# A planned kernel's order redone: q's sixteen transfers as single jobs, one conversion step as two jobs, the first pair's squares on ScalarE, twelve softmax products on GpSimd

## The chip, the cores and the metric

The kernel runs on one core of a Trainium2 chip. The metric is the device time of one execution in microseconds (us), lower is better. Engines are named as in the profile: PE is TensorE's matmul side, PEld its weight load, DVE is VectorE, ACT is ScalarE, POOL is GpSimd, SP is SyncE, which in this kernel computes nothing and issues every DMA in order.

## The reference, cut to what matters

Local attention over chunks of 64 tokens, then two MLPs, all on 4608 tokens (8 batches of 576) with 512 channels (8 heads of 64):

```
scores = scale * q_c @ k_c^T                  # within a chunk of 64 tokens
attn   = exp(scores - max)
attn   = attn / (attn.sum(-1) + 1e-9)
x = (attn @ v_c) -> [4608, 512]
h = relu(x @ w_in)                            # 512 -> 2048
x = (h * h) @ w_out                           # 2048 -> 512
gate = sigmoid(x @ w_gate); val = x @ w_val   # 512 -> 1536
out = (gate * val) @ w_out2                   # 1536 -> 512
```

Inputs arrive in 64-bit words; the weights are turned into float32 on the chip by several instructions of ACT, DVE and POOL.

## The kernel before, in words

The program is not written in the order in which it runs. Python code creates jobs (a job is one engine's work with its inputs and outputs), a planner gives each job a due time, counted back from the nominal times of the matmul jobs, and walks through time placing jobs on the engines and buffers in one large arena of SBUF. The chip then executes the order that came out, one fixed queue per engine, with semaphores for every dependence. What the chip sees of a change of the planner's inputs is thus an order and a choice of buffers.

The attention is done for 36 tiles of 128 tokens. For a tile, PE transposes k and q (line 816; from tile 12 on DVE turns q instead, out of a buffer `ql`), makes the scores S (L836), DVE takes the maximum and subtracts it (L862, L864), ACT takes the exponential (L867), DVE sums it (L868), adds the 1e-9 (L871), takes the reciprocal (L872) and multiplies the 128x512 tile by it (L873). PE transposes the result (T, L880), ACT copies it out of PSUM (`aT`, L427), PE multiplies by v (X, L896), and ACT writes the result into `raw` (L914). The table `TIMES` holds a nominal time for k, q, S, T and X of each tile.

Three tiles make a block of 384 tokens, two blocks make a pair; there are six pairs. The first product (512 -> 2048) runs pair by pair, in eight groups of weights. The first pair is done plainly, 32 output blocks; each is read out of PSUM by ACT with a relu into a buffer `e`, squared, and stored to DRAM (`gd`). The other pairs use seven products for eight, with sums and differences of inputs and outputs (`B..`, `T..` are token operands, `wia`, `wit`, `wis`, `wid` weight operands, `b`, `c`, `e`, `h` output buffers that are stored to `gd`). Every operand is kept as a high and a low part, the low part made by DVE (L447), and each product is three passes (L649, three matmuls of 128x384). Weights `w` are made from `wraw` by ACT (L489, L493), DVE (L496, L498, L505) and POOL (L512). While one pair's products run, the attention of the next pair is threaded between them, so PE alternates between L649 and the attention's lines. From about 360 us on there is no attention left. A later stage (L1031) then does the rest.

`ql` is filled by `load_turned`: sixteen small transfers, one for each head pair and quarter of the partitions, that were one job. There are eleven such fillings. `gd<-e` and the like are the stores of an output buffer, also issued by SP; a buffer is written again only after its store has landed. `ACTF.Square` is ACT's square, `binary("DVE", ..., ALU.mult, ...)` the same on DVE with one operand in PSUM (L456).

Of the kernel before, what the change touches and what calls it, by code (L numbers as in the profile page):

```python
# [39 lines left out]
class Buf:  # L40
    def __init__(self, size=0, top=False, name="", psum=False, op=False):
        self.size, self.top, self.name, self.psum, self.op = size, top, name, psum, op
        self.writers, self.readers, self.users = [], [], 0
        self.at = None


class Job:
    __slots__ = ("eng", "cost", "emit", "deps", "succ", "left", "bufs", "allocs", "lag",
                 "n", "due", "nominal", "start", "end", "stream", "bytes", "look", "started", "shared")


class Plan:
# [3 lines left out]
    def job(self, eng, cost, emit, reads=(), writes=(), stream=None, size=0, soon=None, look=None, at=None, shared=False):  # L56
        j = Job()
        j.shared = shared
# [9 lines left out]
        for b in writes:  # L68
            j.deps.update(b.writers)
            j.deps.update(b.readers)  # L70
# [11 lines left out]
        j.allocs = [b for b in writes if (b.size or b.psum) and b.users == 1]  # L82
# [6 lines left out]
    def due(self):  # L89
# [29 lines left out]
    def run(self):  # L119
# [105 lines left out]
        while done < len(jobs):  # L225
            moved = True
            while moved:
                moved = False
                for e in engines:
# [23 lines left out]
                    while ready[e] and tries < 600:  # L253
# [5 lines left out]
                        if need and ok:  # L259
                            if due - t + shift > (j.look or (self.LOOK if e == "SP" else self.NEAR)):  # L260
                                ok = False
                            else:
                                held = 0
                                for d, m in wants:
                                    if d >= due or d > t - shift + self.HOLD:
                                        break
                                    if not jobs[m].started:
                                        held += sum(b.size for b in jobs[m].allocs if b.at is None)
# [69 lines left out]
def tile_attention_relu2_glu(  # L338
# [77 lines left out]
    def dma(out_, in_, reads=(), writes=(), size=0, n=1, soon=None, look=None):  # L416
# [5 lines left out]
        return job("SP", 0.45 * n, go, reads, writes, size=size, soon=soon, look=look)  # L422
# [46 lines left out]
    def to_float32(src, name, look=None, raws=None):  # L469
# [24 lines left out]

        def three():
            nc.vector.tensor_scalar_max(at(w), at(w), TINY)  # L496
# [19 lines left out]
        job("DVE", 0.8, three, [w], [w], shared=True)  # L516
# [193 lines left out]
    LOOK_QK = 40.0  # L710
# [18 lines left out]
    def load_turned(nm, g):  # L729
# [4 lines left out]
        def both():  # L734
            x = at(r).rearrange("p (h i d) -> p h i d", h=HP, d=32)
            o, i = [], []
            for g4 in range(4):
                part = slice(32 * g4, 32 * g4 + 32)
                cols = slice(32 * (g4 % 2), 32 * (g4 % 2) + 32)
                for hp in range(HP):  # L740
                    o.append(x[part, hp])
                    i.append(src[b, 2 * hp + g4 // 2, s:s + GROUP * 32, cols].rearrange("(i t) d -> t i d", t=32))
            return o, i

        dma(lambda: both()[0], lambda: both()[1], writes=[r], size=P * HP * GROUP * 32 * 8, n=16, look=LOOK_QK)

    def turn_round(nm, t, o):
# [23 lines left out]
        (-2.5, -2.25, 3.5, 9.5, 12.5),  # L771
        (2.25, -4.75, 24.5, 15, 5.5),
        (5.75, 10.25, 5.75, 10.25, 19.75),
        (11.75, 7.5, 13, 28.5, 24.75),
        (22.25, 18.5, 20.5, 17, 37),
        (41.25, 44.75, 41.75, 42.5, 50.75),
        (64.25, None, 63, 73.5, 74.5),
        (78, None, 77.5, 81.5, 83.25),
        (84, None, 82, 89, 94.25),
        (101, None, 98, 106.75, 106),  # L780
        (84.75, None, 93.5, 122.25, 108.25),
        (105.25, None, 107.5, 105.75, 110.5),
        (125, None, 120, 125.75, 142),
        (113, None, 119.5, 124.5, 127.25),
        (125, None, 128, 150.75, 155.75),
        (146.781, None, 147.822, 153.027, 157.191),
        (152.75, None, 158.5, 160, 170),
        (158.5, None, 163.5, 167, 183.5),
        (182.75, None, 185.25, 192.5, 190.25),
        (192.25, None, 192.5, 200, 194.75),  # L790
        (197.25, None, 199.5, 203.25, 209),
        (194.75, None, 201.5, 203.25, 200),
        (205.25, None, 211.25, 219.75, 219.75),
        (216.5, None, 225.25, 234.75, 229),
        (247, None, 242.75, 254.5, 261.5),
        (259.5, None, 253.75, 269.25, 275.25),
# [594 lines left out]
```

## Time and profile before

| | |
|---|---|
| median of 3 runs | 1624.57 us (1623.97 to 1626.49) |
| the profiled execution's own time | 1623.55 us |
| its span | 1621.5 us (2.05 us lie outside the span) |
| mean granted clock of PE | 0.995 of full speed |
| PE busy | 1590.0 us, 98% of the span |
| DVE busy | 1325.2 us, 82% |
| ACT busy | 971.5 us, 60% |
| POOL busy | 524.8 us, 32% |

Busy is the time in which an engine executed an instruction, over one profiled execution. The span begins at the first and ends at the last instruction. In a row of a timeline, the bracket at the end holds the idle time of that engine just before the instruction and what ended it.

### The profile page before, as it was taken

The page shows a single profiled execution, that of the slowest core. Times are in us where ns is not written, and L with a number is a line of the kernel's source. Part 1 is how long each engine was busy: PE and PEld are TensorE (multiplying, and loading weights), DVE is VectorE, ACT ScalarE, POOL GpSimd, SP SyncE. Part 2 cuts the span into 40 slices and gives each one's busy share as a digit, 9 for nine tenths or more (in the row PEclk, how much of TensorE's full clock was granted, in tenths as well). Part 3 has the DMA queues.
Part 4 walks back from the last instruction along what each step waited for, and adds up shares of the span by engine and source line. Part 5 has one row for each costly group of instructions (what it writes and reads, how often), then busy time and mean ns, then how long its engine had stood idle before and what let it go on. Part 6 is the DMA issues. An engine that isn't in the chain of part 4 may idle for free.

```text
span 1621.5 us, 30663 instructions
## 1 busy us (share of the span) xinstructions
PE 1590.0 (98%) x10500; PEld 1442.0 (89%) x10500; DVE 1325.2 (82%) x2290; ACT 971.5 (60%) x1968; POOL 524.8 (32%) x420
## 2 busy tenths in 40 slices
PE   7999999999999999999999999999999999999998
PEld 5898998999999999999998898888888888888887
DVE  7997977878899999999998696835776748889886
ACT  7875756666776666566665555534564545555553
POOL 0253402030442114021157685624676531000000
PEclk9999999999999999999999999999999999999999
DMA  9874667676885676686787556486536577876562
GB/s 219 248 182 117 155 162 189 192 199 198 278 283 194 216 239 201 217 283 209 256 282 262 192 174 228 157 270 230 174 145 218 184 260 252 235 193 169 144 171 47
DMA packets 390796, 333.34 MB, mean 206 GB/s; under 512 B 234736, under 2 KB 325616, under 8 KB 390640
## 3 DMA queue, kind: packets, MB, share of 16 engines
q1 hardware_dynamic: 390640, 331.38, 67.0%
q8 instruction: 83, 1.36, 0.3%
q14 instruction: 73, 0.60, 0.1%
HBM read 209.13 MB, written 122.16 MB: 204 GB/s over the span
## 4 chain that ended last, share of the span: by engine, by line
PE 73%; DVE 2%; issue 1%; POOL 1%; ACT 0%; DMA 0%; SPq 0%; DVEq 0%; POOLq 0%; ACTq 0%
PE bank L1031 37%; PE bank L649 35%; PE bank L896 0%; PE bank L836 0%; DMA w__5725<-wf 0%; POOL ws__5872 L456 0%; POOL ws__5810 L456 0%; DVE T__1990 L447 0%; PE bank L880 0%; DMA g__6317<-gd 0%; POOL ws__7199 L456 0%; DVE T__1983 L447 0%; DVE b__4956 L456 0%; ACT c__3874 L427 0%; POOL wf__7139 L512 0%
## 5 line engine op out<-in xcount | busy, mean ns | idle before, releaser
L512 POOL TENSOR_TENSOR wf__6765<-wf__6765,wr__6689 128x512 int32<-128x512 int32 x18 | 36.4, 2023 | 170.0 <-DVE wf__6765 L505 52.7
L512 POOL TENSOR_TENSOR wf__3460<-wf__3460,wr__3365 128x512 int32<-128x512 int32 x16 | 21.5, 1341 | 172.5 <-DVE wf__3460 L505 65.9
L512 POOL TENSOR_TENSOR wf__7139<-wf__7139,wr__6689 128x512 int32<-128x512 int32 x18 | 28.0, 1558 | 115.4 <-DVE wf__7139 L505 73.6
L456 POOL TENSOR_TENSOR raw__501<-raw__677,raw__501 128x384 f32<-128x384 f32 x20 | 23.5, 1192 | 37.4 <-ACT raw__677 L914 14.2
L493 ACT ACTIVATE wr__6689<-wr__6689 128x512 int32<-128x512 uint32 x36 | 24.0, 667 | 0.0
L447 DVE TENSOR_TENSOR wx__7277<-ws__7199,wx__7277 128x512 fp32r<-128x512 f32 x18 | 19.0, 1054 | 3.9 <-ACT wx__7277 L442 3.9
L447 DVE TENSOR_TENSOR wx__7082<-ws__7199,wx__7082 128x512 fp32r<-128x512 f32 x18 | 18.0, 999 | 4.9 <-ACT wx__7082 L442 4.9
L496 DVE TENSOR_SCALAR wf__7139<-wf__7139 128x512 f32<-128x512 f32 x18 | 11.9, 659 | 7.0 <-ACT wf__7139 L489 7.0
L456 POOL TENSOR_TENSOR ws__7199<-ws__7199,wf__6765 128x256 f32<-128x256 f32 x18 | 16.2, 898 | 1.3
L496 DVE TENSOR_SCALAR wf__6765<-wf__6765 128x512 f32<-128x512 f32 x18 | 11.5, 641 | 6.1 <-ACT wf__6765 L489 6.0
L489 ACT ACTIVATE wf__3460<-wr__3365 128x512 f32<-128x512 f32 x16 | 10.7, 670 | 9.2 <-DMA wf<-wf__3460 6.3
L456 POOL TENSOR_TENSOR ws__7199<-wf__6765,wf__7139 128x256 f32<-128x256 f32 x18 | 15.5, 863 | 0.3
L505 DVE SCALAR_TENSOR_TENSOR wf__7139<-wr__6689,wf__7139 128x512 int32<-128x512 int32 x18 | 15.4, 856 | 0.2
L442 ACT ACTIVATE wx__7204<-wf__7139 128x256 fp32r<-128x256 f32 x18 | 7.4, 413 | 12.2 <-POOL wf__7139 L512 12.2
L447 DVE TENSOR_TENSOR wx__7204<-wf__7139,wx__7204 128x256 fp32r<-128x256 f32 x18 | 14.0, 778 | 0.6 <-ACT wx__7204 L442 0.5
L496 DVE TENSOR_SCALAR wf__3460<-wf__3460 128x512 f32<-128x512 f32 x16 | 7.3, 456 | 8.5 <-ACT wf__3460 L489 7.2
L489 ACT ACTIVATE wf__6765<-wr__6689 128x512 f32<-128x512 f32 x18 | 11.9, 661 | 3.0 <-POOL ws__7199 L456 1.1
L505 DVE SCALAR_TENSOR_TENSOR wf__6765<-wr__6689,wf__6765 128x512 int32<-128x512 int32 x18 | 13.3, 740 | 0.2
L427 ACT ACTIVATE c__12027<-bank 128x512 f32<-128x512 f32 x8 | 4.8, 597 | 14.0 <-PE bank L649 14.0
L498 DVE TENSOR_SCALAR wf__6765<-wf__6765 128x512 int32<-128x512 int32 x18 | 12.6, 698 | 0.6
L456 POOL TENSOR_TENSOR raw__501<-raw__501 128x384 f32<-128x384 f32 x10 | 13.0, 1323 | 0.0
L489 ACT ACTIVATE wf__7139<-wr__6689 128x512 f32<-128x512 f32 x18 | 11.9, 659 | 1.6 <-DMA wr__6689<-in_moe_w_val_dram 0.8
(5940 smaller groups left out, 6120.9 us busy)
## 6 DMA issues: line engine op xcount, KB each, us to landing
ad<-wx__7082 SPq DMA_DIRECT2D x27, 512.0 KB, 5.0
ad<-wx__7277 SPq DMA_DIRECT2D x27, 512.0 KB, 4.7
wr__3365<-in_moe_w_out_dram SPq DMA_DIRECT2D x16, 512.0 KB, 4.4
wr__6689<-in_moe_w_gate_dram SPq DMA_DIRECT2D x12, 512.0 KB, 4.2
wr__6689<-in_moe_w_val_dram SPq DMA_DIRECT2D x12, 512.0 KB, 4.4
wr__6689<-in_moe_w_out_dram SPq DMA_DIRECT2D x12, 512.0 KB, 3.9
ad<-wx__7204 SPq DMA_DIRECT2D x18, 256.0 KB, 4.0
wf<-wf__3460 SPq DMA_DIRECT2D x16, 256.0 KB, 4.4
```

What stands on the lines that cost most here:

```text
L427: lambda: nc.scalar.activation(out=o(), in_=i(), func=func, **kw), ib, ob, soon=soon,
L442: lambda: nc.scalar.activation(out=hi(), in_=at(src, n, F32, off), func=ACTF.Copy),
L447: lambda: nc.vector.tensor_tensor(out=lo(), in0=at(src, n, F32, off), in1=hi().bitcast(F32), op=ALU.subtract),
L456: eng, cost(eng, n), lambda: e.tensor_tensor(out=o(), in0=a(), in1=b(), op=op),
L489: nc.scalar.activation(out=at(w), in_=t[:, :, 1].bitcast(F32), func=ACTF.Abs)
L493: nc.scalar.activation(out=low, in_=low.bitcast(U32), func=ACTF.Copy, scale=2.0**-29)
L496: nc.vector.tensor_scalar_max(at(w), at(w), TINY)
L498: nc.vector.tensor_scalar(out=wi, in0=wi, scalar1=5, scalar2=2, op0=ALU.logical_shift_left, op1=ALU.logical_shift_right,)
L505: nc.vector.scalar_tensor_tensor(out=wi, in0=words()[:, :, 1], scalar=-0x40000000, in1=wi, op0=ALU.bitwise_and, op1=ALU.bitwise_or,)
L512: nc.gpsimd.tensor_tensor(out=wi, in0=wi, in1=words()[:, :, 0], op=ALU.add)
L649: nc.tensor.matmul(out=o, lhsT=at(op, P, F32R, wi * size + half * HB + kk * P), rhs=at(xb, n, F32R, xi * xsize + off), start=(first and kk ...
L1031: nc.tensor.matmul(out=at(ps[m], n), lhsT=at(w, P, F32R, wi * size + half * HB + m * P), rhs=at(x, n, F32R, xi * n), start=(first and kp = ...
```

## The change

Five edits, all in how jobs are made; which products are computed stays as it was.

1. Each of the sixteen transfers that fill `ql` is a job of its own, with a slightly higher cost and a lead of 10 in its due time, so that the planner may put other DMAs between them. The buffer is marked as written in parts, so the sixteen don't wait for one another.
2. The weights' conversion step of two DVE instructions (maximum, then integer scale) becomes two jobs, between which other DVE work may come.
3. In the first pair, the 16 output blocks that DVE squared are squared by ACT, as the other 16 were.
4. The softmax step of three DVE instructions becomes two jobs: the add and the reciprocal on DVE, and the product, for tiles 0 to 11 on POOL, for the others on DVE.
5. The table `TIMES` has other values for most tiles from 6 on.

```
@@ dma
-    def dma(out_, in_, reads=(), writes=(), size=0, n=1, soon=None, look=None):
+    def dma(out_, in_, reads=(), writes=(), size=0, n=1, soon=None, look=None, lead=0.0, cost=0.45):
...
-        return job("SP", 0.45 * n, go, reads, writes, size=size, soon=soon, look=look)
+        return job("SP", cost * n, go, reads, writes, size=size, soon=soon, look=look, lead=lead)
@@ Plan.due
-            extra = self.DMA_LATENCY + self.MARGIN + j.bytes / 200e3 if j.eng == "SP" else 0.4
+            extra = self.DMA_LATENCY + self.MARGIN + j.bytes / 200e3 + j.lead if j.eng == "SP" else 0.4
@@ to_float32
+        def bound():
+            nc.vector.tensor_scalar_max(at(w), at(w), TINY)
+
         def three():
-            nc.vector.tensor_scalar_max(at(w), at(w), TINY)
...
-        job("DVE", 0.8, three, [w], [w], shared=True)
+        job("DVE", 0.41, bound, [w], [w], shared=True)
+        job("DVE", 0.41, three, [w], [w], shared=True)
@@ load_turned
+        r.parts = True
+        for hp in range(HP):
             for g4 in range(4):
...
-        dma(lambda: both()[0], lambda: both()[1], writes=[r], size=P * HP * GROUP * 32 * 8, n=16, look=LOOK_QK)
+                dma(lambda g4=g4, hp=hp: to(g4, hp), lambda g4=g4, hp=hp: of(g4, hp), writes=[r],
+                    size=32 * GROUP * 32 * 8, look=LOOK_QK, lead=LEAD_QK, cost=0.55)
@@ TIMES (k, q, S, T, X of tiles 6 and 7)
-        (-2.5, -2.25, 3.5, 9.5, 12.5),
-        (2.25, -4.75, 24.5, 15, 5.5),
...
+        (-1.75, 4, 5.75, 0.75, 20.5),
+        (2.5, -1.25, -0.25, -2, 11.5),
...
@@ attention
-        def norm():
+        def inverse():
             nc.vector.tensor_scalar_add(col8(mx, 1), col8(mx, 1), 1e-9)
             nc.vector.reciprocal(out=col8(mx, 1), in_=col8(mx, 1))
-            nc.vector.tensor_tensor(out=heads(a), in0=heads(a), in1=col8(mx, 1).to_broadcast([P, H, CH]), op=ALU.mult)
-
-        job("DVE", 1.05, norm, [a, mx], [a, mx], shared=True)
+
+        job("DVE", 0.3, inverse, [mx], [mx], shared=True)
+        eng = "POOL" if t < BY_POOL else "DVE"
+        binary(eng, lambda: heads(a), lambda: heads(a), lambda: col8(mx, 1).to_broadcast([P, H, CH]), ALU.mult,
+               BLK, [a], [a, mx])
@@ finish0
-                if row == col:
-                    binary("DVE", u.words(t), u.words(ps), u.words(t), ALU.mult, n, [t], [t, ps])
-                else:
-                    copy(u.words(t), [t], u.words(t), [t], n, func=ACTF.Square, soon=4.0)
+                copy(u.words(t), [t], u.words(t), [t], n, func=ACTF.Square, soon=4.0)
```

In the orders below, a name is followed by its place in the arena and a number. The first place is VectorE's queue just ahead of the first product. `B` and `T` are the low parts of token operands, `w` weights in conversion (L496, L498, L505 before; L499, L503, L510 after), `wia` the low part of the first product's weight operand. Before:

```order
L873 TENSOR_TENSOR a_14336__636<-a_14336__636,mx_0__370 128x512
L447 TENSOR_TENSOR B_3072_204800__638<-raw_6144_94208__501,B_3072_204800__638 128x384
L496 TENSOR_SCALAR w_28672__687<-w_28672__687 128x512
L498 TENSOR_SCALAR w_28672__687<-w_28672__687 128x512
L505 SCALAR_TENSOR_TENSOR w_28672__687<-wraw_10240__581,w_28672__687 128x512
L447 TENSOR_TENSOR B_3072_201728__644<-raw_6144_94208__501,B_3072_201728__644 128x384
L496 TENSOR_SCALAR w_0__718<-w_0__718 128x512
L498 TENSOR_SCALAR w_0__718<-w_0__718 128x512
L505 SCALAR_TENSOR_TENSOR w_0__718<-wraw_18432__624,w_0__718 128x512
L447 TENSOR_TENSOR wia_83968__756<-w_28672__687,wia_83968__756 128x512
L447 TENSOR_TENSOR B_3072_198656__668<-raw_6144_94208__501,B_3072_198656__668 128x384
```

After, the same place on VectorE:

```order
L880 RECIPROCAL mx_0__370<-mx_0__370 128x8
L450 TENSOR_TENSOR B_3072_201728__692<-raw_6144_94208__512,B_3072_201728__692 128x384
L499 TENSOR_SCALAR w_512__706<-w_512__706 128x512
L503 TENSOR_SCALAR w_512__706<-w_512__706 128x512
L510 SCALAR_TENSOR_TENSOR w_512__706<-wraw_10240__577,w_512__706 128x512
L499 TENSOR_SCALAR w_6656__712<-w_6656__712 128x512
L503 TENSOR_SCALAR w_6656__712<-w_6656__712 128x512
L510 SCALAR_TENSOR_TENSOR w_6656__712<-wraw_14336__612,w_6656__712 128x512
L450 TENSOR_TENSOR B_3072_198656__731<-raw_6144_94208__512,B_3072_198656__731 128x384
L450 TENSOR_TENSOR wia_83968__758<-w_512__706,wia_83968__758 128x512
```

The six products of L873 are gone from this queue, here the last of them; the fourth `B` now stands ahead of `wia`. The six products stand on POOL, ahead of the first weight's conversion there.

The second place is SP's queue around the end of the first pair; `gd<-e` are stores, all other rows loads. Before, `e_8192` and `e_2048` are buffers of the last group of the first pair:

```order
L420 DMA gd_87<-e_32768__1871 128x384
L420 DMA gd_95<-e_18432__1114 128x384
L420 DMA ql_19968__1500<-in_q_dram 32x9x32 x16
L420 DMA gd_95<-e_8192__1695 128x384
L420 DMA gd_87<-e_2048__1904 128x384
L420 DMA v_0__2038<-in_v_dram 128x8x64
```

After:

```order
L423 DMA gd_86<-e_32256__1815 128x384
L423 DMA gd_94<-e_26624__1361 128x384
L423 DMA k_6656__1846<-in_k_dram 128x8x64
L423 DMA v_65536__1857<-in_v_dram 128x8x64
L423 DMA ql_12800__1437<-in_q_dram 32x9x32 x16
L423 DMA gd_87<-e_38912__1468 128x384
L423 DMA gd_95<-e_26624__1361 128x384
L423 DMA gd_87<-e_51200__1291 128x384
L423 DMA gd_95<-e_67584__1937 128x384
```

The sixteen transfers still stand in one run, now ahead of all four stores of the pair's last group (two to `gd_87`, two to `gd_95`), where before two of these four stood ahead of it and two behind. One run of sixteen is what nine of the eleven fillings show; the first filling has other DMAs between its sixteen, and the second has one store between them.

The third place is SP's queue around the end of the second pair of the seven-product kind (`b`, `c`, `e` and `h` are output buffers, `wr` and `wf` the next stage's weights). Before:

```order
L420 DMA gd_93<-b_15872__3579 128x384
L420 DMA gd_86<-e_36352__3670 128x384
L420 DMA ql_22016__3250<-in_q_dram 32x9x32 x16
L420 DMA gd_93<-h_30720__2471 128x384
L420 DMA wr_2048__3365<-in_moe_w_out_dram 128x1024
L420 DMA gd_85<-c_14336__3375 128x384
L420 DMA wf_208<-wf_9728__3460 128x512
L420 DMA gd_94<-b_8192__3706 128x384
```

After:

```order
L423 DMA wr_67584__3077<-in_moe_w_out_dram 128x1024
L423 DMA ql_14848__3780<-in_q_dram 32x9x32 x16
L423 DMA gd_93<-h_28672__3711 128x384
L423 DMA gd_94<-b_0__2780 128x384
L423 DMA gd_87<-e_51200__1291 128x384
L423 DMA gd_94<-h_1536__3815 128x384
L423 DMA gd_86<-c_63488__2573 128x384
L423 DMA wf_210<-wf_12800__3144 128x512
L423 DMA gd_95<-b_65024__3793 128x384
```

The run of sixteen stands just ahead of `gd_93<-h` in both; the store of `c` that was third behind it is `gd_85`, which after the change is no longer behind it, and the stores behind it now belong to a later time.

## Rows read from the trace of the kernel before

**Rows 1.** Windows: busy time of each engine, granted clock, DMA share, GB/s.

```profile
core 0: us, PE busy (x) PEld busy (x) DVE busy (x) ACT busy (x) POOL busy (x), PEclk, DMA share, GB/s
20.00:40.00 20.00, 15.44 (x285) 12.47 (x278) 19.18 (x40) 18.05 (x41) 2.94 (x2) 0.91 1.08 250
120.00:140.00 20.00, 17.31 (x179) 15.79 (x178) 16.11 (x34) 9.80 (x23) 6.82 (x6) 0.91 0.52 124
280.00:300.00 20.00, 19.42 (x164) 18.77 (x164) 17.03 (x37) 14.29 (x32) 1.30 (x1) 0.91 0.51 160
0.00:364.00 364.00, 341.39 (x3702) 318.73 (x3702) 297.36 (x585) 248.48 (x539) 99.79 (x94) 0.99 0.73 185
```

**Rows 2.** PE's waits from 0 to 360 us: releaser, total, times, longest.

```profile
PE bank L649 <- ACT aT__2078 L427: 2.6, 1, 2.6
PE bank L649 <- DVE b__3816 L456: 2.3, 1, 2.3
PE bank L880 <- ACT e__1135 L427: 0.9, 1, 0.9
PE bank L880 <- DVE a__989 L873: 0.5, 1, 0.5
PE bank L880 <- DVE a__2427 L873: 0.3, 1, 0.3
```

**Rows 3.** SP's timeline at the two places: start, duration, operation, count.

```profile
120.69 9.04 SPq L420 DMA_DIRECT2D ql__1500<-in_q_dram  x16
129.84 0.40 SPq L420 DMA_DIRECT2D gd<-e__1695  x1
...
262.08 10.12 SPq L420 DMA_DIRECT2D ql__3250<-in_q_dram  x16
...
273.28 0.40 SPq L420 DMA_DIRECT2D gd<-c__3375  x1
```

**Rows 4.** ACT's timeline: the copies that wait for those stores.

```profile
131.98 0.49 ACT L427 ACTIVATE e__1695<-bank 128x384 f32<-128x384 f32 x1 [3.77 <-DMA gd<-e__1695]
...
278.98 0.49 ACT L427 ACTIVATE e__3900<-bank 128x384 f32<-128x384 f32 x1 [2.77 <-DMA gd<-c__3375]
```

**Rows 5.** PE's timeline: the first product's start, then two pairs' first products.

```profile
35.39 0.61 PE L649 MATMUL bank<-B__633,wia__756 128*128 128x384 f32 x2 [0.97 <-DVE wia__756 L447]
...
120.92 0.79 PE L649 MATMUL bank<-B__633,wia__756 128*128 128x384 f32 x3
...
272.89 0.68 PE L649 MATMUL bank<-B__633,wia__756 128*128 128x384 f32 x3
```

**Rows 6.** VectorE's timeline: a softmax product, a conversion, a square.

```profile
28.84 0.69 DVE L873 TENSOR_TENSOR a__636<-a__636,mx__370 128x512 f32<-128x512 f32 x1
...
32.03 1.52 DVE L496 TENSOR_SCALAR w__718<-w__718 128x512 f32<-128x512 f32 x1
33.58 0.43 DVE L498 TENSOR_SCALAR w__718<-w__718 128x512 int32<-128x512 int32 x1
...
122.69 0.55 DVE L456 TENSOR_TENSOR e__1695<-bank,e__1695 128x384 f32<-128x384 f32 x1
```

**Rows 7.** GpSimd's timeline: a conversion's last step, and two float32 subtractions.

```profile
31.87 1.39 POOL L512 TENSOR_TENSOR w__687<-w__687,wraw__581 128x512 int32<-128x512 int32 x1 [30.57 <-DMA q__685<-in_q_dram]
...
115.41 2.55 POOL L456 TENSOR_TENSOR raw__501<-raw__677,raw__501 128x384 f32<-128x384 f32 x2 [2.24 <-DVE B__633 L447]
```

**Rows 8.** PE's timeline: products with one, and with two attention steps between them.

```profile
65.47 0.68 PE L649 MATMUL bank<-B__644,wit__1169 128*128 128x384 f32 x3
65.99 0.69 PE L649 MATMUL bank<-B__668,wit__1169 128*128 128x384 f32 x3
...
67.87 0.68 PE L649 MATMUL bank<-T__781,wia__1099 128*128 128x384 f32 x3
...
79.28 0.68 PE L649 MATMUL bank<-B__825,wia__1253 128*128 128x384 f32 x3
...
81.62 0.68 PE L649 MATMUL bank<-T__781,wit__1302 128*128 128x384 f32 x3
```

More of the change, by code (lines that the diff above doesn't have):

```diff
@@ L43, in __init__ @@
         self.writers, self.readers, self.users = [], [], 0
-        self.at = None
+        self.at, self.parts = None, False
 class Job:
     __slots__ = ("eng", "cost", "emit", "deps", "succ", "left", "bufs", "allocs", "lag",
-                 "n", "due", "nominal", "start", "end", "stream", "bytes", "look", "started", "shared")
+                 "n", "due", "lead", "nominal", "start", "end", "stream", "bytes", "look", "started", "shared")
 class Plan:
@@ L54, in __init__, with job @@
         self.jobs, self.room, self.first = [], room, []
-    def job(self, eng, cost, emit, reads=(), writes=(), stream=None, size=0, soon=None, look=None, at=None, shared=False):
+    def job(self, eng, cost, emit, reads=(), writes=(), stream=None, size=0, soon=None, look=None, at=None, shared=False, lead=0.0):
         j = Job()
+        j.lead = lead
         j.shared = shared
@@ L68, in job @@
         for b in writes:
-            j.deps.update(b.writers)
+            if not b.parts:
+                j.deps.update(b.writers)
             j.deps.update(b.readers)
@@ L81, in job @@
             j.bufs.append(b)
-        j.allocs = [b for b in writes if (b.size or b.psum) and b.users == 1]
+        j.allocs = [b for b in writes if (b.size or b.psum) and (b.users == 1 or b.parts)]
         j.started = False
@@ L267, in run @@
                                     if not jobs[m].started:
-                                        held += sum(b.size for b in jobs[m].allocs if b.at is None)
+                                        others.update(b for b in jobs[m].allocs if b.at is None)
+                                held = sum(b.size for b in others)
                                 if due - t + shift > self.FAR:
@@ L732, in load_turned, with to, of @@
         b, s = divmod(g * GROUP * 32, S)
-        def both():
+        def to(g4, hp):
             x = at(r).rearrange("p (h i d) -> p h i d", h=HP, d=32)
-            o, i = [], []
-            for g4 in range(4):
[L738 to L743, printed above, removed]
-        dma(lambda: both()[0], lambda: both()[1], writes=[r], size=P * HP * GROUP * 32 * 8, n=16, look=LOOK_QK)
+            return x[32 * g4:32 * g4 + 32, hp]
+        def of(g4, hp):
+            cols = slice(32 * (g4 % 2), 32 * (g4 % 2) + 32)
+            return src[b, 2 * hp + g4 // 2, s:s + GROUP * 32, cols].rearrange("(i t) d -> t i d", t=32)
+        r.parts = True
+        for hp in range(HP):
+            for g4 in range(4):
+                dma(lambda g4=g4, hp=hp: to(g4, hp), lambda g4=g4, hp=hp: of(g4, hp), writes=[r],
+                    size=32 * GROUP * 32 * 8, look=LOOK_QK, lead=LEAD_QK, cost=0.55)
     def turn_round(nm, t, o):
@@ new lines, in tile_attention_relu2_glu @@
+        (178.75, None, 183, 181.75, 187),
+        (191.5, None, 191.75, 193.75, 202.5),
+        (201, None, 204.5, 211.25, 212.75),
+        (206.5, None, 200.25, 207.5, 216.75),
+        (217.75, None, 219.75, 223.75, 219.75),
+        (217.25, None, 224.25, 234, 231.25),
+        (241.512, None, 242.553, 247.758, 251.922),
+        (248.799, None, 249.84, 255.045, 259.209),
+        (256.086, None, 257.127, 262.332, 266.496),
+        (263.373, None, 264.414, 269.619, 273.783),
+        (273.75, None, 280.5, 288.25, 290.5),
```

48 lines of the change are left out of this document (19 added, 29 removed).

## The prediction, made before the changed kernel ran

> **What bounds the kernel now.** I read the windows first, to see where PE is not working. From 0 to 364 us PE is busy 341.39 us [rows 1]; of its 31.5 idle us in the whole span (1621.5 less 1590.0, from the table) 22.6 lie there, though it is less than a quarter of the span. The two orders differ on PE only in the attention's steps, and those end about there, so later stages can change little: the result is decided by PE's waits before 360 us. Part of these 22.6 us passes before the first loads are there, which no edit touches. The list of waits [rows 2] names the largest of the later ones: 2.6 us for `aT__2078` and 2.3 us for `b__3816`. Neither releaser is the cause. The windows show a second price: in 120 to 140 us and in 280 to 300 us the granted clock is 0.91 on the mean, though PE had work [rows 1]: a mix of its two levels, 2.4 and 1.2 GHz. Each of the two windows holds one of these two waits, so I lay the fall to them and price it at 0.09 x 20 = 1.8 us each.
>
> Then SP's and ACT's timelines tell what was late. At 120.69 SP starts sixteen transfers of `ql` in one run, 9.04 us long, and only at 129.84 the store of `e__1695` [rows 3]. ACT, idle for 3.77 us, can write `e__1695` again at 131.98 [rows 4]: the store took 2.14 us to land. So ACT was free at 128.2, the buffer was late by those 3.77 us, and behind that copy stand ACT's parts of `T__2062`, `T__2069` and `aT__2078`, for which PE waits. The pair's first product began at 120.92 [rows 5], so the run of sixteen started 0.2 us ahead of the pair. The second place is not quite the same: the run began at 262.08, 10.8 us ahead of the pair's start at 272.89, and the store of `c__3375` went out at 273.28 [rows 3, 5], but ACT got the buffer only at 278.98 [rows 4], 5.7 us later, not 2.14. By the order the load of `wr` stands between the run and that store; the run made both late together and the store landed behind the load.
>
> **The change part by part.** *q's transfers.* Sixteen transfers cost SP as much as before, 9.04/16 = 0.565 us each; what counts is what stands behind them. The order says that in nine of eleven fillings nothing stands between them. What moved is the run. At the first place it now stands ahead of all four last stores of the first pair. It waits for its buffer, which a transpose of q on DVE frees. Counting the products that PE has between that transpose and the pair's start (about 5.5 us), I place the run's start 5.5 us ahead of the pair's start instead of 0.2, its end 3.6 us behind it, and the landing of the first store at 3.6 + 2.1 = 5.7 us. The first output of the new pair that needs such a buffer is wanted at about 5.9 us, where before it was wanted at 128.2 - 120.92 = 7.3 and landed at 11.1. So it should just be in time, with 0.2 us to spare: the stall of 2.6 us goes, and with it the 1.8 us of clock, **-4.4 us** (bounds -4.4 and 0). At the second place `c`'s store and `wr` both stand ahead of the run; the run starts at the latest 7.3 us ahead of the pair's start, ends 1.8 us behind it, and the stores behind it are out, at 0.40 us each and a little between them, by 6.2. The first buffer is wanted at about 4.4 and lands at 4.7, the next is wanted at 7.3 and lands by about 6.5. I take this stall as gone too: 2.3 + 1.8 = **-4.1 us** (bounds -4.1 and 0). Both times are estimates, from the counted order and these rows.
>
> *The products on GpSimd.* One took DVE 0.69 us [rows 6]. No row has it on POOL. A 128x512 int32 step took POOL 1.39 us, two 128x384 float32 steps 2.55 us, which at 512 columns makes 2.55/2 x 4/3 = 1.70 [rows 7]. I take 1.5, between them, since it is the same engine and one operand is a broadcast of eight columns. So every one of the twelve chains from S to T grows by 0.8 us, while DVE is relieved of 12 x 0.69 = 8.3 us. For the first six tiles that pays where DVE is the engine that is late: in 20 to 40 us it is busy 19.18 of 20 us, and PE's first product waited 0.97 us for `wia`, up to 35.39 [rows 1, 5]. Six products are 4.1 us of DVE's time, but not all comes back: `wia` now stands behind the second weight's conversion and the fourth `B`, ACT is itself busy 18.05 of these 20 us, and the loads of the last tiles don't come earlier. I take what this wait is worth and a little, **-1.1 us** (bounds -2.5, a start at 33, and +1.0, `wia` behind one more stretched conversion as in the next paragraph). For the other six the chain in tiles 6 and 7 (6.9 and 6.7 us between S and T by PE's order, as against 4.4 + 0.8 for the work) is still covered on paper, but other work stands between on DVE: **+1.0 us** (0 to 2).
>
> *The port.* At 32.03 a conversion took DVE 1.52 us, the next step of the same size 0.43, and it lies inside POOL's step from 31.87 to 33.26 [rows 6, 7]: the two engines don't run freely beside each other. In the Trainium skill, SBUF — State Buffer, section Who interferes with whom, the two share a port pair as an exclusive lock, reductions never take it, and an instruction of DVE contends when both its inputs lie in SBUF; the row agrees as far as one conversion goes. By the page the reductions and the subtractions out of PSUM that fill DVE's queue beside the first six products would run on, and the start's -1.1 would stand. By the row alone each of the twelve products may stretch one DVE instruction by 1.1 us, in place of the 0.69 us that it takes off; for the first six that would be 6 x 0.4 = 2.5 us later instead of 1.1 earlier. I keep the -1.1, since most of what stands beside the first six is of another form than that row, and hold the other as a rival (D).
>
> *Squares.* Sixteen at 0.55 us leave DVE [rows 6], 8.8 us, and add about as much to ACT, which in 0 to 364 us is idle for 364 - 248.48 = 115 us [rows 1]. Cost nothing; what hides it is that idle time. If ACT were full at one of them, a bank would be freed some 0.5 us later. *Conversion in two jobs*: the same instructions, nothing. *Lead and cost* act through the order alone.
>
> *TIMES.* The new order has 37 separate places with attention's S or X between products in place of 40. One alone costs PE 67.87 - 65.99 - 2 x 0.52 = 0.84 us, two together 81.62 - 79.28 - 2 x 0.52 = 1.30, where 0.52 is a product's step (65.99 - 65.47) [rows 8]: joining two saves 0.38, three times **-1.1 us**. Against it, S and T stand at most 6 us apart in 14 tiles instead of 10. Of those ten three waited, 0.9, 0.5 and 0.3 us [rows 2], 0.17 us per tile; four more make **+0.7 us**.
>
> Sum: -4.4 - 4.1 - 1.1 + 1.0 - 1.1 + 0.7 = -8.9 us. From the profiled execution's 1623.55 us that is 1614.7; the median lies 1.02 us above that execution, so **1616 us**.
>
> **The rivals.** *A, 0.52*: as summed, 1612 to 1620. *B, the run of sixteen is still a run, 0.17*: that the transfers are ordered singly and yet stand together in nine of eleven fillings speaks for it, and my slack of 0.2 us at the first place and -0.3 at the second; against it, the stores wanted next are further off. One stall back is 1620, both 1624. *C, slower, 0.13*: softmax chains. If the 14 tight tiles each wait, T comes late again and again, and PE has nothing in reserve, since its queue is fixed. The sum without the +0.7 is -9.6, so it decides from 9.6/14 = 0.69 us per tile, and makes the kernel slower by 0.2% from 0.92, some 1628 to 1630. For it: one of the old ones waited 0.9 us; against: seven of ten waited for nothing, and DVE is relieved of 28 instructions. *D, GpSimd gives nothing, 0.09*: each product stretches a DVE instruction by 1.1 us and saves 0.69, 12 x 0.4 = 4.9 us more of DVE's time instead of 8.3 less; with the start's 1.1 lost and all 4.9 on the path, 1622. For it the row at 32.03; against it, the first six stand at a time when POOL has nothing else (2.94 us busy in 20 to 40 us [rows 1]) and DVE mostly reads PSUM or reduces. The Trainium skill, Perfetto Trace Analysis, section Optimizing Scalar/DVE Operations, warns that moving work between these two "might not help", as they share a port; no run here has yet shown it for this step. *E, more than that, 0.09*: waits like the 0.9 and 0.5 us of [rows 2] vanish too as DVE gets air, and the start gives its 2.5, with a few more of that size: 1609.
>
> **How the numbers follow.** The likeliest is A. About 0.2%, 3.25 us, is what a measurement of this kernel can tell from no change, so faster is below 1621.3 and slower above 1627.8. Faster: most of A (0.49), E (0.09), the half of B with one stall (0.07), a little of D (0.02), 0.67. Same: 0.03 of A, 0.08 of B, 0.06 of D, 0.02 of C, 0.19. Slower: the rest of C (0.11), of B (0.02) and of D (0.01), 0.14. The range for 8 in 10 reaches from 1608, where E and the start's bound of -2.5 lie, to 1625, where both stalls are back; A alone is 1612 to 1620.
>
> **What would show it.** Right: no wait over 2 us behind a run of `ql` between 110 and 290 us, ACT's first copies of those pairs without a wait for `gd<-..`, the clock at 1.00 in both windows; PE's first product at 34.1 to 34.5; a POOL product near 1.5 us. Wrong: a new wait of PE for ACT or DVE of over 1 us with a store as ACT's releaser (B); many waits of T (L890) for the product (C); DVE's conversions at 1.5 us beside POOL's products and a first product later than 35.4 (D).

## The result, and the profile after

The changed kernel takes 1609.7 us (median of 4 runs, 1608.33 to 1611.15) against 1624.27 in the same comparison: a ratio of 0.9908, interval 0.9891 to 0.9925. A second comparison on another chip gave 0.9922 (0.9909 to 0.9935). So it is faster by 13 to 15 us, where the prediction said 8.6; the time lies in the range, next to case E (1609) and below case A (1612 to 1620). The profiled execution took 1608.33 us.

The profile's page after, busy time, share of the span, instructions:

```profile
span 1606.6 us, 30680 instructions
PE 1582.9 (99%) x10500; PEld 1440.2 (90%) x10500; DVE 1313.9 (82%) x2262; ACT 979.8 (61%) x1984; POOL 534.5 (33%) x432
```

PE's busy time fell by 7.1 us and its idle time by 7.8. Part of the busy time that went is clock: the windows after, to be read beside [rows 1],

```profile
20.00:40.00 20.00, 14.99 (x251) 12.48 (x251) 15.91 (x34) 16.72 (x38) 6.03 (x6) 0.83 1.00 244
120.00:140.00 20.00, 19.50 (x172) 18.32 (x171) 17.57 (x38) 12.87 (x28) 6.74 (x6) 1.00 0.41 119
280.00:300.00 20.00, 19.69 (x258) 18.67 (x257) 17.67 (x40) 11.42 (x25) 1.31 (x1) 1.00 0.76 201
```

show full clock where it was 0.91 in two places, and a lower one than before at the start. At the start the clock differs between executions of one order: the five traces of before's order in this document have 0.91 or 0.83 there, the seven of the changed order 0.75 to 0.91. PE's largest waits from 0 to 360 us after, for [rows 2], without one of 4.2 us for the very first load, which before had too:

```profile
PE bank L890 <- POOL a__644 L459: 2.4, 1, 2.4
PE bank L890 <- POOL a__374 L459: 1.6, 1, 1.6
PE bank L906 <- ACT aT__589 L430: 1.2, 1, 1.2
PE bank L655 <- DVE b__2780 L459: 1.0, 1, 1.0
PE bank L824 <- DMA k__648<-in_k_dram: 0.9, 1, 0.9
PE bank L655 <- ACT c__4800 L430: 0.8, 1, 0.8
```

The waits for `aT` and `b` at the two pairs' ends are gone. Four of the six that are left lie ahead of the first product. PE's timeline after, for [rows 5]: two waits ahead of the start, the first two products, pair 1's start, the product behind the last attention step, and the last product:

```profile
29.91 1.12 PE L890 MATMUL bank<-ident,a__644 128*128 128x128 f32 x4 [2.39 <-POOL a__644 L459]
...
31.97 1.11 PE L824 MATMUL bank<-ident,k__648 128*128 128x128 f32 x4 [0.95 <-DMA k__648<-in_k_dram]
...
35.77 1.17 PE L655 MATMUL bank<-B__638,wia__758 128*128 128x384 f32 x3
36.77 0.70 PE L655 MATMUL bank<-B__646,wia__758 128*128 128x384 f32 x3
...
119.47 0.77 PE L655 MATMUL bank<-B__638,wia__758 128*128 128x384 f32 x3
...
405.32 0.79 PE L655 MATMUL bank<-T__1996,wit__1562 128*128 128x384 f32 x3
...
1598.95 0.88 PE L1041 MATMUL bank<-x__16486,o__14839 128*128 128x256 f32 x6
```

The same places before, with the transpose of the sixth tile's product ahead of the start (`a__636` before, `a__644` after):

```profile
29.59 1.11 PE L880 MATMUL bank<-ident,a__636 128*128 128x128 f32 x4
...
33.98 0.44 PE L649 MATMUL bank<-B__633,wia__756 128*128 128x384 f32 x1
...
35.84 0.69 PE L649 MATMUL bank<-B__638,wia__756 128*128 128x384 f32 x3
...
416.23 0.79 PE L649 MATMUL bank<-T__2026,wit__1627 128*128 128x384 f32 x3
...
1613.43 0.88 PE L1031 MATMUL bank<-x__16573,o__14861 128*128 128x256 f32 x6
```

Before, the first product began at 33.98, but stopped for its low weight part up to 35.39 [rows 5]. The second product is the fair mark: it came 0.9 us later than before, the product behind the last attention step 10.9 us earlier, and the last one 14.5. The attention ends later than was said above: its last step on PE began at 415.65 us before and at 404.74 after, and PE's order is the same row by row only from 413 us before, 402 after. Two parts of the result were not foreseen: the start went the other way, and 3.6 us were won behind the attention, where PE's order is the same.

The end of the first pair, on SP after, for [rows 3]:

```profile
115.03 8.13 SPq L423 DMA_DIRECT2D ql__1437<-in_q_dram  x16
123.26 0.40 SPq L423 DMA_DIRECT2D gd<-e__1468  x1
123.76 1.46 SPq L423 DMA_DIRECT2D gd<-e__1361  x1
```

and ACT's copy into the buffer of `e__1468`, for [rows 4]:

```profile
126.53 0.50 ACT L430 ACTIVATE c__2018<-bank 128x384 f32<-128x384 f32 x1 [0.24 <-PE bank L655]
```

The run began 4.4 us ahead of the pair (5.5 estimated), and ACT waited for PE, not for a store.

### The profile page after: what moved, and what is told of

Read it like the earlier page. It is cut to its first block, busy times and chain, and to the rows that moved or that the text cites. A ratio compares the mean times of both kernels' runs of the same rounds, so it can differ in the third digit from the quotient of the medians.

```text
span 1606.6 us, 30680 instructions
## 1 busy us (share of the span) xinstructions
PE 1582.9 (99%) x10500; PEld 1440.2 (90%) x10500; DVE 1313.9 (82%) x2262; ACT 979.8 (61%) x1984; POOL 534.5 (33%) x432
## 4 chain that ended last, share of the span: by engine, by line
PE 92%; DVE 2%; issue 1%; ACT 1%; DMA 1%; SPq 0%; POOL 0%; DVEq 0%; ACTq 0%; POOLq 0%
PE bank L655 52%; PE bank L1041 37%; PE bank L844 1%; PE bank L906 1%; PE bank L890 1%; PE bank L824 1%; DMA ad<-wx__7306 0%; DMA w__1305<-wf 0%; SPq L423 0%; DMA ql__3981<-in_q_dram 0%; DVE B__731 L450 0%; POOL a__880 L459 0%; DVE e__5615 L1141 0%; DVE T__1978 L450 0%; DVE mx__1969 L876 0%
## 5 line engine op out<-in xcount | busy, mean ns | idle before, releaser
L517 POOL TENSOR_TENSOR wf__6764<-wf__6764,wr__6699 128x512 int32<-128x512 int32 x18 | 32.9, 1830 | 170.1 <-DVE wf__6764 L510 139.7
L517 POOL TENSOR_TENSOR wf__3144<-wf__3144,wr__3077 128x512 int32<-128x512 int32 x16 | 21.6, 1352 | 162.3 <-DVE wf__3144 L510 100.9
L517 POOL TENSOR_TENSOR wf__7149<-wf__7149,wr__6699 128x512 int32<-128x512 int32 x18 | 27.2, 1512 | 122.4 <-DVE wf__7149 L510 78.3
L496 ACT ACTIVATE wr__6699<-wr__6699 128x512 int32<-128x512 uint32 x36 | 24.0, 668 | 0.0
L450 DVE TENSOR_TENSOR wx__7306<-ws__5829,wx__7306 128x512 fp32r<-128x512 f32 x18 | 18.4, 1023 | 4.2 <-ACT wx__7306 L445 4.2
L450 DVE TENSOR_TENSOR wx__7092<-ws__5829,wx__7092 128x512 fp32r<-128x512 f32 x18 | 16.8, 932 | 5.6 <-ACT wx__7092 L445 5.6
L499 DVE TENSOR_SCALAR wf__7149<-wf__7149 128x512 f32<-128x512 f32 x18 | 11.0, 613 | 12.3 <-ACT wf__7149 L492 12.3
L510 DVE SCALAR_TENSOR_TENSOR wf__6764<-wr__6699,wf__6764 128x512 int32<-128x512 int32 x18 | 16.0, 891 | 0.3
L450 DVE TENSOR_TENSOR wx__7219<-wf__7149,wx__7219 128x256 fp32r<-128x256 f32 x18 | 14.2, 791 | 1.6 <-ACT wx__7219 L445 1.6
L499 DVE TENSOR_SCALAR wf__6764<-wf__6764 128x512 f32<-128x512 f32 x18 | 10.1, 560 | 6.5 <-ACT wf__6764 L492 6.5
L510 DVE SCALAR_TENSOR_TENSOR wf__7149<-wr__6699,wf__7149 128x512 int32<-128x512 int32 x18 | 15.1, 838 | 0.3
L870 DVE TENSOR_REDUCE mx__370<-bank 128x4 f32<-128x256 f32 x16 | 6.6, 415 | 10.2 <-PE bank L844 10.2
L499 DVE TENSOR_SCALAR wf__3144<-wf__3144 128x512 f32<-128x512 f32 x16 | 7.5, 468 | 8.8 <-ACT wf__3144 L492 8.8
L924 ACT ACTIVATE raw__695<-bank 128x256 f32<-128x256 f32 x36 | 11.7, 392 | 3.8 <-PE bank L906 3.7
L924 ACT ACTIVATE raw__512<-bank 128x256 f32<-128x256 f32 x36 | 12.1, 382 | 2.4 <-PE bank L906 2.1
L870 DVE TENSOR_REDUCE mx__1969<-bank 128x4 f32<-128x256 f32 x16 | 6.7, 418 | 8.1 <-PE bank L844 8.0
```

The lines of the kernel that those rows point to most:

```text
L450: lambda: nc.vector.tensor_tensor(out=lo(), in0=at(src, n, F32, off), in1=hi().bitcast(F32), op=ALU.subtract),
L496: nc.scalar.activation(out=low, in_=low.bitcast(U32), func=ACTF.Copy, scale=2.0**-29)
L510: nc.vector.scalar_tensor_tensor(out=wi, in0=words()[:, :, 1], scalar=-0x40000000, in1=wi, op0=ALU.bitwise_and, op1=ALU.bitwise_or,)
L517: nc.gpsimd.tensor_tensor(out=wi, in0=wi, in1=words()[:, :, 0], op=ALU.add)
L924: nc.scalar.activation(out=o[:, :, a:a + CH], in_=i, func=ACTF.Copy)
```

## The experiments

Two kinds were made. Where an edit goes into the planner's input, everything is placed anew. So most experiments keep the order that was planned and change one thing in it afterwards: the place of a run of transfers, or the engine that executes a step. Before took 1621.6, 1622.8 and 1622.35 us in the three comparisons behind the first, so each kernel is read as a ratio to before on its own chip.

**The run of sixteen behind two stores, in the order of before.** `put_behind` takes the sixteen transfers of one filling of `ql` out of the finished order and puts them behind SP's next jobs; its first number counts the fillings from 0, the second those jobs.

```
         plan.run()
+        put_behind(2, 2)
         plan.emit()
```

> The kernel before with one thing moved: at the end of the first pair the run of sixteen q transfers stands behind the two stores that followed it; nothing is planned anew. If the run holds the stores back in SP's queue (the prediction's reading), the wait for aT (2.6 us) and ACT's wait of 3.8 us for the store are gone, the granted clock is 1.00 from 120 to 140 us, and the time is 4.4 us shorter, about 1620 us. Rival: the store was late for another reason (the DMA engines, or the next buffers in turn), then a wait of 2 to 3 us stays near 133 us and the time is within 1 us of before.

Ratio 0.9979 (0.9970 to 0.9989), 1618.6 us. SP's timeline of this kernel, and below it a window:

```profile
123.71 0.32 SPq L420 DMA_DIRECT2D gd<-e__1695  x1
124.08 0.42 SPq L420 DMA_DIRECT2D gd<-e__1904  x1
124.55 9.52 SPq L420 DMA_DIRECT2D ql__1500<-in_q_dram  x16
```

```profile
120.00:140.00 20.00, 19.24 (x200) 18.23 (x199) 16.92 (x35) 12.45 (x29) 6.41 (x6) 1.00 0.59 147
```

The store of `e__1695` went out 6.1 us earlier, the wait for `aT` is gone, the clock is full. Between the products at 126.36 and 139.32 us of before, this trace gained 4.4 us on it, and 3.7 from the pair's first product on; the ratio gives 3.4 (1.8 to 4.9). The reading of the first place is shown.

**The same at the second place.** `put_behind(7, 3)`.

> The kernel before with the run of sixteen q transfers at the end of the third pair put behind the three DMAs that followed it (a store of h, the load of wr, the store of c). If the run made the store of c late, the wait for b (2.3 us) and the low clock from 280 to 300 us go, 4.1 us, about 1620 us. Rival: c's store landed late because of the load of wr ahead of it, or wr itself waits for its buffer and holds SP up: then a wait of over 1 us stays and the time changes by less than 1 us, or grows.

Ratio 1.0001 (0.9992 to 1.0010). PE's waits there in this kernel, in its timeline:

```profile
277.82 0.79 PE L649 MATMUL bank<-T__2062,wid__2746 128*128 128x384 f32 x3 [0.67 <-DVE b__3800 L456]
...
282.88 0.79 PE L649 MATMUL bank<-T__2026,wit__800 128*128 128x384 f32 x3 [0.60 <-ACT c__3749 L427]
...
297.34 0.69 PE L836 MATMUL bank<-kT__2588,qT__3434 64*64 64x64 f32 x32 [0.49 <-DVE qT__3434 L759]
```

The wait of 2.3 us shrank to 0.7 and the clock stayed at 1.00 in both windows from 260 to 300 us. But two new waits of 0.6 and 0.5 us came within 20 us, the second for a turned q. ACT's timeline shows why so little changed:

```profile
277.83 0.68 ACT L489 ACTIVATE wf__3460<-wr__3365 128x512 f32<-128x512 f32 x1 [2.78 <-DMA wf<-wf__3460]
```

ACT no longer waits for `c`'s store (2.77 us in [rows 4]), but 2.78 us for the store of `wf`, which stood next in SP's queue and is now the one behind the run; the copies of `b` and `c` for which PE waits stand behind that in ACT's queue. Neither theory held: the run did make the store late, yet taking that away in the old order is worth nothing that the comparison can tell. Between the products at 254.03 and 348.21 us of before, this trace won 2.0 us on it; but the three other traces of before's order, which leave this place alone, won 0.9, 1.0 and 2.1 there too, so the profiled execution of before lost more here than others of its order do. They have the same wait, of 1.8 to 2.1 us, and in one of them, that with the squares on ScalarE, the clock stayed at 1.00 from 260 to 300 us.

**Products on GpSimd, squares on ScalarE, in the order of before.** Two kernels:

```
-            nc.vector.tensor_tensor(out=heads(a), ... op=ALU.mult)
+            eng = nc.gpsimd if t < 12 else nc.vector
+            eng.tensor_tensor(out=heads(a), ... op=ALU.mult)
```

> The kernel before in its own order, with the twelve softmax products given to GpSimd and nothing planned anew. By the prediction's prices (1.5 us on GpSimd for 0.69 on VectorE, the start up to 1.1 us earlier, chains of tiles 6 to 11 longer by 0.8 us): between 1623 and 1627 us. Rival, each product stretches a VectorE instruction by 1.1 us: first product later than 36 us, 1628 to 1630. Rival, VectorE's queue was what made the first pair late: 1621 or less.

```
                 if row == col:
                     binary("DVE", u.words(t), u.words(ps), u.words(t), ALU.mult, n, [t], [t, ps])
+                    plan.jobs[-1].emit = lambda: nc.scalar.activation(out=at(t, n), in_=at(t, n), func=ACTF.Square)
```

> The kernel before in its own order, with the sixteen VectorE squares of the first pair given to ScalarE and nothing planned anew. By the prediction: no change, 1623.5 to 1625.5 us. Rival: the first pair's waits come from VectorE being full from 40 to 120 us, then some of the 0.9 and 0.5 us waits go and it is 1 to 2 us faster. Rival: ScalarE becomes late with its copies, 2 to 7 us slower.

Ratios 1.0004 (0.9995 to 1.0013) and 1.0000 (0.9991 to 1.0009). Each edit alone, in the old order, is worth nothing.

**The table alone, and all but the table**, both planned anew; beside them the changed kernel again.

> The changed kernel again, beside the three others on one chip: 0.991 of before, as in its first timing (0.989 to 0.9925).

> The kernel before with the changed table TIMES alone, planned anew; the other four edits are left out. If the table brings most of the gain (products and squares alone brought nothing in the runs so far): 10 us faster or more, 1611 or less where before takes 1621.6. Rival: the table was made for the work as the other edits divide it and does not suit the old division: VectorE late from 34 to 120 us, within 3 us of before or slower.

> The changed kernel with the old table TIMES, planned anew: the transfers ordered singly, conversion, squares and products as changed. If the table brings most: within 3 us of before. Rival: the four other edits bring most of it: 8 us or more faster than before.

Ratios 0.9922 (0.9909 to 0.9935), 1.0147 (1.0133 to 1.0162) and 1.0942 (1.0928 to 1.0957): 24 us and 153 us slower than before. Neither theory had such sizes. The largest waits of the table alone, 0 to 230 us, without that for the very first load:

```profile
PE bank L880 <- DVE a__2335 L873: 4.4, 1, 4.4
PE bank L836 <- DVE qT__2147 L759: 2.6, 1, 2.6
PE bank L649 <- ACT wis__2397 L442: 2.4, 1, 2.4
```

For all but the table, PE's timeline shows one wait and ACT's timeline its making:

```profile
250.42 1.13 PE L844 MATMUL bank<-kT__2023,qT__1603 64*64 64x64 f32 x32 [126.42 <-ACT kT__2023 L430]
```

```profile
141.54 0.66 ACT L492 ACTIVATE wf__1754<-wr__1646 128x512 f32<-128x512 f32 x1 [8.84 <-DMA wf<-wf__1754]
...
150.35 0.66 ACT L492 ACTIVATE wf__1754<-wr__1646 128x512 f32<-128x512 f32 x1 [7.59 <-DMA wf<-wf__1754]
...
249.77 0.60 ACT L430 ACTIVATE kT__2023<-bank 128x512 f32<-128x512 f32 x1 [2.62 <-POOL wf__1754 L517]
```

On ACT's queue fourteen conversions of the next stage's weights stood ahead of one copy that PE needed, and they share one buffer `wf`: thirteen of them waited 7.3 to 8.8 us each for the last one's store, and came some 8.7 us apart. So the edits and the table are not parts with prices of their own.

**The run two stores later, in the order of the changed kernel.** `put_behind(2, 2)` there.

> The changed kernel in its own order, only the run of sixteen q transfers at the end of the first pair put two stores later, so that two of the last group's four stores stand ahead of it and two behind, as before the change. If the place of that run is what makes the stall of the first pair's end: 3 to 4.4 us slower than the changed kernel, with a store as the cause of a wait over 2 us near 130 us. Rival: the buffers in more places carry it: within 1 us of the changed kernel.

Ratio 0.9925 (0.9911 to 0.9939), 1609.63 us: no change. SP's timeline of this kernel:

```profile
119.95 0.34 SPq L423 DMA_DIRECT2D gd<-e__1361  x1
120.38 9.12 SPq L423 DMA_DIRECT2D ql__1437<-in_q_dram  x16
129.59 0.40 SPq L423 DMA_DIRECT2D gd<-e__1291  x1
```

Two stores went out only at 129.6 and later, as late as before the change, and nobody waited: the two of the last group's buffers that the new pair writes first, `e__1468` and `e__1361`, had been stored ahead of the run. The next experiment puts those two behind it.

```
+        moved = [*run, first, second]
+        at_ = order.index(third)
+        plan.order = [j for j in order[:at_ + 1] if j not in moved] + moved + order[at_ + 1:]
```

> The changed kernel in its own order, with the run of sixteen q transfers at the end of the first pair put where it begins about 0.5 us ahead of the next pair, as before the change, and with the stores of e_38912 and e_26624, the two buffers that the new pair writes first, behind it. If what counts is that the store of a buffer that is wanted next stands behind the run: ACT waits 3 to 4 us for a store, PE 2 to 3 us, the clock falls, 3.5 to 4.4 us slower than the changed kernel, ratio to before 0.994 to 0.995. Rival: the changed order has room for it, within 1 us of the changed kernel.

1612.48 us, ratio 0.9937 (0.9924 to 0.9949). SP's, ACT's and PE's timelines of this kernel:

```profile
120.14 8.95 SPq L423 DMA_DIRECT2D ql__1437<-in_q_dram  x16
129.13 0.45 SPq L423 DMA_DIRECT2D gd<-e__1468  x1
```

```profile
131.41 0.49 ACT L430 ACTIVATE c__2018<-bank 128x384 f32<-128x384 f32 x1 [4.37 <-DMA gd<-e__1468]
```

```profile
131.96 1.33 PE L655 MATMUL bank<-T__1996,wit__779 128*128 128x384 f32 x3 [2.23 <-ACT c__2018 L430]
```

The old picture is back with other names, and the window 120 to 140 us shows 0.91 again. This trace loses 4.4 us at the place against that of the changed kernel; by ratios the loss is some 2.5 us, with intervals that overlap, so its size in the median is less sure than in the trace.

**The changed kernel's order with products, or squares, back on VectorE.**

```
+        if t < 12:                                  # in the other kernel: t < 6
+            plan.jobs[-1].emit = lambda: nc.vector.tensor_tensor(
+                out=heads(a), in0=heads(a), in1=col8(mx, 1).to_broadcast([P, H, CH]), op=ALU.mult)
```

> The changed kernel in its own order, with the softmax products of tiles 0 to 5 given back to VectorE and nothing planned anew; tiles 6 to 11 stay on GpSimd. If GpSimd's products made the start late (waits of 1.6 and 2.4 us for them, then a low clock): the first product 1 to 2 us earlier and the kernel 1 to 2 us faster than the changed one, 0.990 to 0.991 of before where the changed one has 0.992. Rival: VectorE is late again at the start, the first product no earlier, same time.

> The changed kernel in its own order, all twelve softmax products on VectorE and nothing planned anew. If moving them was worth something in this order (VectorE free where it was full): 2 to 8 us slower than the changed kernel. If, as in the order of before, it is worth nothing: within 1.5 us of the changed kernel, and the gain lies in the order.

Ratios 0.9923 (0.9909 to 0.9936) and 0.9919 (0.9905 to 0.9932): no change. With all twelve on VectorE, the wait ahead of the start was

```profile
PE bank L893 <- DVE a__644 L887: 2.3, 1, 2.3
```

nearly the same wait with another releaser, so GpSimd did not make it.

```
                 copy(u.words(t), [t], u.words(t), [t], n, func=ACTF.Square, soon=4.0)
+                if row == col:
+                    plan.jobs[-1].emit = lambda: nc.vector.tensor_tensor(
+                        out=at(t, n), in0=at(t, n), in1=at(t, n), op=ALU.mult)
```

> The changed kernel in its own order, sixteen of the first pair's squares on VectorE (both operands in SBUF) and nothing planned anew. If the room on VectorE that the squares left is what the new order lives on: 2 to 8 us slower than the changed kernel, with waits of PE for VectorE between 60 and 120 us. Rival: nothing, within 1.5 us.

Ratio 0.9938 (0.9925 to 0.9952), 1612.84 us, 3.0 us above the kernel with the products back, in the same comparison. From 80 to 100 us this kernel shows

```profile
80.00:100.00 20.00, 18.12 (x137) 17.38 (x136) 18.78 (x33) 15.57 (x30) 9.01 (x8) 1.00 0.66 169
```

and the changed kernel

```profile
80.00:100.00 20.00, 20.00 (x205) 19.30 (x204) 16.20 (x25) 18.09 (x39) 12.46 (x11) 1.00 0.69 180
```

PE is busy 18.12 us where the changed kernel has 20.00, DVE 18.78 where it has 16.20. Between the products at 62 and 95 us of the changed kernel this trace loses 3.3 us. PE's two larger waits there, 0.7 and 1.2 us, end on ACT and on GpSimd, not on VectorE as expected; the second is for a softmax product for which GpSimd itself waited 0.44 us for VectorE's reciprocal. So the new order does live on the squares being away from VectorE. How much of that is their time alone is less sure: these squares read both inputs from SBUF and took 0.66 us on the mean, up to 1.10, where those of before read one from PSUM and took 0.55; no run separates the two.

## Why the prediction was right, and where it was not

The direction was right, and the stalls at the two places went as forecast; what each was worth, and the rest of the gain, came out otherwise. In the terms of its sum, from the two traces (a place's gain is what one trace wins on the other between the products ahead of it and behind it):

| term | predicted | traces |
|---|---|---|
| start | -1.1 | +0.9 (second product) |
| first pair's end | -4.4 | -4.4 when made alone (ratio: 3.4); gone after |
| second place | -4.1 | gone after; worth nothing alone |
| products, tight chains, joined steps | +0.6 | about -3.3, the rest up to the last attention step |
| later stages | 0 | -3.6 |
| sum | -8.9 | -14.5 at the last product |

The rest of -3.3 is -10.9, less +0.9 and the two places at their predicted 4.4 and 4.1; it is a difference, not a measurement. The predicted terms add up to -9.0, where -8.9 was written; that changes nothing. That the time came out beside case E is luck: E rested on the waits of 0.9 and 0.5 us of [rows 2], which did vanish, and on a start that gives 2.5 us, which it did not, while the 3.6 us of the later stages were put at nothing.

*First place.* The mechanism holds: a store queued behind the run, wanted by the pair's first outputs. But the prediction took the run's start for what decides. The two experiments on the changed order show that it takes two things together, a late run and a wanted store behind it: a late run costs nothing if the buffers wanted next are stored ahead of it. My 0.2 us of slack was too little as well: the store went out at 123.26, which with the 2.1 us of [rows 3, 4] lands at 125.4, and the buffer was wanted at 126.3 (126.53 less 0.24).

*Second place.* The wait is gone after the change, and the low clock with it, as predicted. That 4.1 us could be booked for it was wrong in the order of before: the next store behind the run made ACT wait as long, small waits took the gain, and the 1.8 us of clock came from one execution, while another with a wait of 1.9 us there kept the full clock.

*Products.* In both orders twelve products on GpSimd are worth nothing that the comparisons can tell, as the ratios 1.0004, and 0.9919 beside 0.9922, show. Rival D's price did not come, but its point stands: the Trainium skill, Perfetto Trace Analysis, section Optimizing Scalar/DVE Operations, says that moving work between these two "might not help", and these ratios agree. The prediction's +1.0 - 1.1 was about that by sum, but its start half was wrong in the old order too, where the products alone left the second product at 35.95 (35.84 before); the other half was not measured by itself. The row at 32.03 that it held for rival D is a step with one input, and says nothing on steps with two.

*Start.* The term failed. VectorE did get air (15.91 us busy in 20 to 40 us, 19.18 before), but it was not the last to arrive. PE waited 2.4 us for tile 5's product, yet that step began only 0.3 us later than before (29.91, 29.59): PE had run out of other work earlier. What made it later lies in the five steps from there to the first product. One waited 0.95 us for the load of a k, and all five took 1.1 us at the low clock, where before three of the five did. ACT waited 2.07 us for PE's output and made the high part of `wia` behind that, at 34.74 (33.29 before), so that was late too. The wait for tile 5 with its product on VectorE shows that GpSimd is not the cause; which move in the new order is, no run here separates.

*Squares.* "Cost nothing" was right in the old order and is wrong in the new one, where giving them back, in the form above, costs 3 us.

*Later stages.* The sentence that failed is "later stages can change little". PE's order behind the attention is the same, but the orders of the engines that feed it are not. One of the small waits of before, in PE's timeline and in VectorE's just ahead of it:

```profile
946.80 0.96 PE L649 MATMUL bank<-T__10904,v__10617 128*128 128x512 f32 x3 [0.65 <-ACT c__11099 L427]
```

```profile
942.00 1.51 DVE L496 TENSOR_SCALAR wf__7139<-wf__7139 128x512 f32<-128x512 f32 x1
943.54 1.40 DVE L498 TENSOR_SCALAR wf__7139<-wf__7139 128x512 int32<-128x512 int32 x1
944.86 0.68 DVE L456 TENSOR_TENSOR c__11008<-c__11008,bank 128x512 f32<-128x512 f32 x1
```

Two steps of a conversion, stretched to 1.51 and 1.40 us (0.43 for such a step in [rows 6]) while GpSimd runs its own from 938 to 946, stand one behind the other, and the add that ACT and PE wait for stands behind both. After the change the two are separate jobs, and at this product there is no wait. That the separation is what helps is argued, not shown: no kernel was run with it undone. By PE's idle time behind the attention, 1.6 us before and 0.7 after, such waits are only 0.9 of the 3.6 us; the rest shows as steps a little longer, at full clock in both, and its cause stays open. The loss appears, at 3.4 to 3.5 us, in all four other traces of before's order. Two of the traces of the changed order, those with the first six products and with the squares back, lose 1.4 and 2.6 us of it again, though what was moved in them lies ahead of 125 us; so the size of this gain is not fixed by PE's order.

What stays open is how the remaining gain divides among the edits. The two planned-anew kernels say that this question may have no answer: the table made for one division of the work costs 24 us in another.

## What to carry to other kernels

When a planner decides the order, price the order that came out, not the edits: of the two edits tried singly, products and squares, neither was worth anything in the old order and one was worth 3 us in the new one, and the table and the edits apart made the kernel slower by 24 and 153 us. For a stall behind a long run of DMAs on one queue, look up whose buffer is wanted next; either its store stands ahead of the run, and the run need not move, or the run ends early enough, as in the changed kernel, where by the estimate above that store landed 0.9 us in time. Then look whose store comes next behind the run: at the second place it took over the wait. A stall's price read from one execution can be that execution's alone. And an equal order on the busiest engine does not mean equal time, if the engines that feed it run in another order.

## What the runs showed of the hardware that was not expected

GpSimd's product of 128x512 float32 with a broadcast operand took 1.04 us beside VectorE's reductions and subtractions out of PSUM, as in the two timelines after the change:

```profile
13.96 1.04 POOL L459 TENSOR_TENSOR a__374<-a__374,mx__370 128x512 f32<-128x512 f32 x1 [12.65 <-DMA k__317<-in_k_dram]
```

```profile
14.14 0.42 DVE L872 TENSOR_TENSOR a__448<-bank,mx__446 128x256 f32<-128x256 f32 x1
```

That is less than the bounds of 1.39 and 1.70 that I took from [rows 7]; later it took up to 1.57, at 48.89, beside a VectorE step with two inputs in SBUF (L450). The Trainium skill, GPSIMD Engine Reference, section 3.1, has 4497 ns for a two-input float32 step of four times the columns, which makes an estimate of 1.12 us; the row is nearer to that than my 1.5. While the clock was low at the start, PE's steps of attention lasted 1.11 instead of 0.6 to 0.7 us. The price of such a wait is not fixed: the same wait of 2.3 to 2.4 us at the start stands in all seven traces of the changed order, with a granted clock from 0.75 to 0.91 between 20 and 40 us.
